# Moving the x value products behind the Wo pass, and extra parts ahead of the memory transposes and of the Wo pass, in a segmented attention kernel

## The chip, the cores and the metric

The kernel runs on one core of one Trainium2 chip. The metric is the device time of one execution in microseconds (us). "Before" is the kernel without the change, "after" the kernel with it.

## The reference, cut to what matters

```python
for s in range(64):                                 # 64 segments, one after the other
    h = concatenate([mem, x[:, 32*s:32*s+32]])      # 8 memory rows + 32 tokens, 640 features
    q, k, v = h @ Wq, h @ Wk, h @ Wv                # 32 heads of 128
    p = softmax(mask(q @ k.T * scale))
    o = (p @ v) @ Wo
    mem = o[:, :8]                                  # the next segment needs this
    outs.append(o[:, 8:])
# around it: layer norm of x, h = x + attention, then layer norm and a gated FFN with a residual
```

The 64 segments form a chain through `mem`: eight rows of scores, value products and the Wo pass have to be ready before the next projections can start. Everything else of a segment can be put into gaps of that chain.

## The kernel before

Each segment is issued in this order for TensorE (PE). The names are those of the code; the line numbers are those that the profile prints.

```python
project(a, ks, 1, (0, 1), (P2, P3), spare=20)          # K, lines 401/384; evicted to tok[0], tok[1]
dma_t(KS..., tokp[0][:, :], [("tok", 0), ("tok", 1)], [("KS",)])   # transpose of K by DMA
pv_x(s - 1, BQ[0])                                     # line 643: x value products of the LAST segment
if fin: fin()                                          # transposes of the extras' queries
norm_x(BQ[0]); trans_ox(); kx_x(q)                     # VectorE; DMA transpose ox -> oT; keys into KX
...
project(a, ks, 0, (0, 1), (P0, P1), spare=20)          # Q, evicted to tok[2], tok[3]
project(a, ks, 2, (0, 1), (P2, P3), (0, 1), spare=8)   # V, first chunks
trans8(tok[2], ..., tok[3], ..., T0)                   # line 421: token transposes of Q
kx_mem(KS[:, :, 0:M], ("KS",))                         # VectorE: memory keys into KX, needs KS
project(a, ks, 2, (0, 1), (P2, P3), (2, 3, 4), spare=12)
...
scores(s)                                              # line 540, needs KX
filler(0); filler(1)                                   # "extras": pieces of K, Q or V of other tokens,
pv_mem(s); norm_om()                                   # or of an extra Wo pass, on banks BQ
filler(2)
trans_om()                                             # line 592: memory transposes, needs om of norm_om
mask_x()
filler(3)
wo_pass(T1, MARKS[s % 4])                              # line 604: 128 matmuls, 256 instructions
to_act(s + 1, ...)                                     # VectorE: the next memory rows into act_r
filler(4)
if evac: evac()                                        # evictions of the extras
```

An instruction list in program order is kept for every engine. `MARKS` says how many PE instructions after the begin of the Wo pass a block of 256 should end (the instruction queue of before brought 201 packets for PE's 51361 matmuls and weight loads, 256 a packet), and `align` reaches that by turning some matmuls that reuse loaded weights into matmuls with a load of their own (`spare`):

```python
PE_FIRST, PE_LINE = 64, 256
MARKS = (104, 64, 92, 92)
...
if op.mark is not None:
    p = (-(at + op.mark)) % line      # instructions to add so that the mark is met
```

In this text s%4 is the class of a segment: classes 0, 1 and 2 have different extras, and the row statistics and loads of x fall into different classes too.

The softmax here doesn't subtract the row's maximum and nothing guards it: scores larger than these inputs give would overflow.

## Time and profile before

| | before |
|---|---|
| median, range of 4 runs | 1217.66 us, 1215.56 to 1220.37 |
| the profiled execution | 1211.88 us, span 1210.1, mean granted clock 0.987 |
| four segments (one of each class), segments 5 to 60 | 60.10 us |

The last row is worked out from the starts of the scores in the timeline: 841.39 us between those of segments 5 and 61, divided by 14.

The page of before: the first line gives busy time and share of every engine, the next two the busy tenths of PE and its granted clock in 40 slices, then the instruction queue (packets, MB, share), and the engines' shares of the chain of work that ended last.

```profile
PE 1110.7 (92%) x27964; PEld 529.5 (44%) x23397; DVE 641.9 (53%) x1648; ACT 328.1 (27%) x684; POOL 285.4 (24%) x567
...
PE   5589999999999999999999999999999987999998
...
PEclk9889999999999999999999999999999999999999
...
q8 instruction: 201, 3.29, 1.1%
...
PE 64%; DMA 11%; DVE 9%; POOL 7%; issue 4%; SPq 3%; ACT 2%; DVEq 0%; POOLq 0%
```

PE is busy nine tenths or more in nearly all slices, and the granted clock was 1.00 from 125 to 965 us (windows view of before). But only 64% of the last-ending chain is PE; DMA, VectorE and GpSimd hold the rest. So PE stands and waits for others, for short times and often. The waits view says for whom (line of the wait, what ended it: us in total, times, longest):

```profile
PE ps L592 <- DVE om L586: 21.1, 63, 1.1
PE ps L421 <- DVE tok L430: 19.3, 26, 1.6
PE ps L401 <- DVE act_r L518: 17.2, 63, 0.7
```

Two of these come 63 times, once at every hand-over from one segment to the next. The timeline of one segment shows their places (start, duration, engine, line, operation, tiles; in brackets the idle time and what ended it):

```profile
823.83 0.62 PE L421 MATMUL ps<-ident,tok 128*128 128x128 bf16 x8 [0.82 <-DVE tok L430]
...
825.78 0.69 PE L540 MATMUL ps<-Qr,KX 128*64 128x40 bf16 x32
...
828.45 0.28 PE L592 MATMUL ps<-ident,om 128*128 128x128 bf16 x2 [0.30 <-DVE om L586]
...
829.12 2.40 PE L604 MATMUL ps<-Wo,oT 128*32 128x160 bf16 x128
831.35 0.39 PE L401 MATMUL ps<-W,act_e 128*32 128x512 bf16 x4
831.56 0.39 PE L384 MATMUL ps<-W,act_e 128*32 128x512 bf16 x4
832.19 0.40 PE L401 MATMUL ps<-W,act_r 128*32 128x512 bf16 x4 [0.24 <-DVE act_r L518]
```

The memory transposes (line 592) stand still 0.30 us for om. Then come two extra groups, the Wo pass at 829.12, two extra groups, and the K projection of the next segment stands still 0.24 us for act_r. At 823.83 the token transposes have waited 0.82 us for tok; in this segment the Kr transpose of the extras' keys held it (VectorE stood 1.31 us for that transfer before it wrote tok at 823.08). The transposes by DMA (times, median us from issue to landing):

```profile
oT<-ox SPq DMA_TRANSPOSE x64, 2.8
KS<-tok SPq DMA_TRANSPOSE x63, 3.1
...
Kr<-tok SPq DMA_TRANSPOSE x15, 5.1
```

### The profile page before, as it was taken

Reading aid. Unit: us, or ns where it says so; the run is one execution under the profiler, and the core shown is the slowest. Engines: PE = TensorE matmul, PEld = TensorE weight load, DVE = VectorE, ACT = ScalarE, POOL = GpSimd, SP = SyncE. Lnnn points to the kernel's source line nnn. Section 1 sums busy time; section 2 is a strip of 40 time slices with the busy share of each in tenths; the row PEclk is TensorE's granted clock in tenths of the full one; section 3 lists DMA queues with packets and bytes.
Section 4 is the critical chain, followed back from the end, with each engine's and each line's share of the span. In section 5 each row is a group of like instructions: output and inputs, shape, how many; then the busy total and the mean of one; then the engine's idle time right before and its main releaser. Section 6 shows DMA issues by size and latency. Waiting matters only on the chain.

```text
span 1210.1 us, 55379 instructions
## 1 busy us (share of the span) xinstructions
PE 1110.7 (92%) x27964; PEld 529.5 (44%) x23397; DVE 641.9 (53%) x1648; ACT 328.1 (27%) x684; POOL 285.4 (24%) x567
## 2 busy tenths in 40 slices
PE   5589999999999999999999999999999987999998
PEld 2344444444444444444444444444444444443443
DVE  3245656565655565566666665565656552543522
ACT  2123232323232323232323232322232321211210
POOL 1013233323233232233232323232323220000000
PEclk9889999999999999999999999999999999999999
DMA  9933333334333434353534343434332359131200
GB/s 357 359 51 68 61 68 61 71 58 73 56 75 54 75 54 75 54 102 56 101 56 101 58 99 56 74 56 73 58 69 58 63 139 252 26 82 44 50 22 22
DMA packets 214103, 102.45 MB, mean 85 GB/s; under 512 B 188032, under 2 KB 203456, under 8 KB 213872
## 3 DMA queue, kind: packets, MB, share of 16 engines
q1 hardware_dynamic: 196016, 82.96, 31.3%
q0 software_dynamic: 17664, 15.94, 6.9%
q8 instruction: 201, 3.29, 1.1%
q14 instruction: 30, 0.25, 0.1%
q10 hardware_dynamic: 192, 0.01, 0.0%
HBM read 36.79 MB, written 7.21 MB: 36 GB/s over the span
## 4 chain that ended last, share of the span: by engine, by line
PE 64%; DMA 11%; DVE 9%; POOL 7%; issue 4%; SPq 3%; ACT 2%; DVEq 0%; POOLq 0%
PE ps L401 16%; PE ps L384 14%; PE ps L604 10%; PE ps L953 9%; POOL Vr L352 5%; DMA Kr<-tok 4%; PE ps L421 3%; PE ps L540 3%; PE ps L986 3%; DMA attn_d<-ox 3%; DMA Wo<-in_A_Wo_dram 2%; SPq L352 2%; PE ps L643 2%; DMA oT<-ox 2%; DVE ox L655 2%
## 5 line engine op out<-in xcount | busy, mean ns | idle before, releaser
L401 PE MATMUL ps<-W,act_r 128*32 128x512 bf16 x4421 | 398.1, 386 | 23.9 <-DVE act_r L518 17.2
L384 PE MATMUL ps<-W,act_r 128*32 128x512 bf16 x3459 | 339.5, 379 | 0.0
L352 POOL DMA_DIRECT2D Vr<-Vp x376 | 188.2, 508 | 481.7 <-ACT Vp L428 284.8
L401 PEld LDWEIGHTS ps<-W,act_r 128*32 128x32 bf16 x4421 | 117.3, 97 | 283.1 <-issue 158.6
L430 DVE CAST tok<-ps 128x512 bf16<-128x512 f32 x161 | 110.8, 688 | 128.7 <-PE ps L384 92.8
L604 PE MATMUL ps<-Wo,oT 128*32 128x160 bf16 x8320 | 162.9, 238 | 12.4 <-DMA Wo<-in_A_Wo_dram 8.4
L604 PEld LDWEIGHTS ps<-Wo,oT 128*32 128x32 bf16 x8320 | 150.8, 99 | 30.6 <-DVE oT L430 17.0
L428 ACT ACTIVATE tok<-ps 128x512 bf16<-128x512 f32 x161 | 96.0, 596 | 242.2 <-PE ps L384 178.4
L428 ACT ACTIVATE Qr<-ps 128x768 bf16<-128x768 bf16 (+3 forms) x110 | 69.2, 658 | 104.2 <-DVE Qr L430 92.7
L428 ACT ACTIVATE wtok<-ps 128x160 bf16<-128x160 f32 x64 | 19.5, 305 | 272.6 <-DVE TBf L517 264.5
L655 DVE TENSOR_TENSOR ox<-ps,rx 128x512 bf16<-128x512 f32 x128 | 82.5, 686 | 17.6 <-DMA attn_d<-ox 15.9
L401 PE MATMUL ps<-W,act_e 128*32 128x512 bf16 x900 | 89.0, 383 | 0.0
L384 PE MATMUL ps<-W,act_e 128*32 128x512 bf16 x900 | 88.1, 379 | 0.0
L517 DVE STREAM_TRANSPOSE TBf<-ps 128x160 f32<-128x160 f32 x64 | 22.4, 350 | 112.2 <-PE ps L604 112.1
L352 POOL DMA_DIRECT2D attn_d<-wtok x64 | 47.6, 744 | 129.1 <-ACT wtok L428 129.1
L421 PE MATMUL ps<-ident,tok 128*128 128x128 bf16 x664 | 51.1, 220 | 19.9 <-DVE tok L430 19.3
L968 DVE TENSOR_TENSOR hT<-g,ps 128x512 bf16<-128x512 bf16 (+1 forms) x56 | 38.5, 688 | 52.6 <-PE ps L953 48.7
L421 PEld LDWEIGHTS ps<-ident,tok 128*128 128x128 bf16 x664 | 37.3, 98 | 64.6 <-DVE tok L430 62.1
L953 PE MATMUL ps<-xn2T,Wg 128*128 128x512 bf16 x260 | 64.7, 379 | 0.0
L953 PE MATMUL ps<-xn2T,Wu 128*128 128x512 bf16 x260 | 64.6, 379 | 0.0
L986 PE MATMUL ps<-Wd,hT 128*128 128x320 bf16 (+1 forms) x240 | 63.3, 300 | 0.0
L430 DVE CAST Vp<-ps 128x512 bf16<-128x512 f32 x64 | 44.3, 692 | 31.6 <-PE ps L384 28.2
(91 smaller groups left out, 1138.2 us busy)
## 6 DMA issues: line engine op xcount, KB each, us to landing
Vr<-Vp POOLq DMA_DIRECT2D x124, 48.8 KB, 1.9
W<-in_A_Wk_dram SPq DMA_DIRECT2D x2, 2560.0 KB, 13.0
W<-in_A_Wq_dram SPq DMA_DIRECT2D x2, 2560.0 KB, 25.1
W<-in_A_Wv_dram SPq DMA_DIRECT2D x2, 2560.0 KB, 26.8
Wo<-in_A_Wo_dram SPq DMA_DIRECT2D x2, 2560.0 KB, 28.6
xt<-in_A_x_dram SPq DMA_DIRECT2D x30, 160.0 KB, 2.6
Vr<-Vp POOLq DMA_DIRECT2D x128, 32.5 KB, 2.3
attn_d<-wtok POOLq DMA_DIRECT2D x64, 40.0 KB, 3.2
```

The costliest lines, as they stand in the source:

```text
L352: add(eng, lambda e: e.dma_start(dst, src), r=r, w=w, dma=True)
L384: return pe.add_instruction(mybir.InstMatmult(name=nc.get_next_instruction_name(), engine=mybir.EngineType.PE, ins=[pe.lower_ap(rhs), pe.l ...
L401: ins = pe.matmul(*a, start=(c == 0), stop=(c == DC - 1), skip_group_check=True)
L421: ins = pe.matmul(bank_bf(b)[:, k * 128:(k + 1) * 128], t[:, (k % 4) * 128:(k % 4 + 1) * 128], ident[:, :], is_transpose=True)
L428: add("act", lambda a: a.activation(dst, src, ACTF.Copy), r=r, w=w)
L430: add("dve", lambda v: v.tensor_copy(dst, src), r=r, w=w)
L540: i = pe.matmul(bank((P0, P1)[e])[64 * cg:64 * cg + 64, 40 * k:40 * k + 40], KX[:, h, :], Qr[:, h, q, :], start=True, stop=True, skip_grou ...
L604: i = pe.matmul(bank(bk)[32 * gg:32 * gg + 32, 0:160], oT[:, hb, :], w[:, gg], start=(hb == 0), stop=(hb == 31), skip_group_check=True)
L655: add("dve", lambda v, kh=kh: v.tensor_tensor(ox[:, kh, :, :], src[:, :, kh, 0:128], ap(rx, kh, [[2, 4], [0, 128]]), ALU.mult), r=[B(b0 + ...
L953: ins = pe.matmul(bank(bk), w[:, c, lo:lo + 128], xn2T[par][:, c, :], start=(c == 0), stop=(c == DC - 1))
L968: add("dve", lambda v: v.tensor_tensor(hT[par][lo:128, j, :], g1[gi][lo:128, :], bank(bu)[lo:128, :], ALU.mult), r=[B(bu), ("g1", gi)], w= ...
L986: i = pe.matmul(*a, start=(j == 0), stop=(j == FC - 1), skip_group_check=True)
```

## The change

Its intent is to put work that waits for nothing where PE waited. It computes the same.

```diff
-    MARKS = (104, 64, 92, 92)
+    MARKS = (204, 164, 192, 192)
...
-            project(a, ks, 1, (0, 1), (P2, P3), spare=20)       # K
-            to_tok(P2, 0, "act")
-            to_tok(P3, 1, "dve")
+            project(a, ks, 1, (0, 1), BQ, spare=20)
+            to_tok(BQ[0], 0, "act")
+            to_tok(BQ[1], 1, "dve")
             dma_t(KS..., tokp[0][:, :], ...)
-            pv_x(s - 1, BQ[0])
-            if fin: fin()
-            norm_x(BQ[0]); trans_ox(); kx_x(q)
-            n = ...; if n: row_scale(...); dma_t(at, xt)
+            for f in late: f()                                  # row statistics put off
             project(a, ks, 0, (0, 1), (P0, P1), spare=20)       # Q
+            n = ...; if n: row_scale(...); dma_t(at, xt)
...
         filler(2)
+        filler(3)
         trans_om()
         mask_x()
-        filler(3)
+        filler(4)
+        if evac: evac()                                         # both evictions on ScalarE now
+        if woe: ...; woe_sum(BQ[0]); woe_store(...)             # by way of `at`, no longer ox
         wo_pass(T1, MARKS[s % 4] if s > 3 else None)
         to_act(s + 1, ...)
...
-        filler(4)
-        if evac: evac()
-        if woe: ...
+        pv_x(s, P0)                                             # x value products of THIS segment
+        if nfin: nfin()
+        norm_x(P0); trans_ox(); kx_x(seg_slot(s + 1))
```

Smaller things come along: half of the score matmuls load 40 instead of 64 weight columns, the row statistics of x and a residual add go to the next segment (`late`), `ln1_back` runs later, and `align` fills its `spare` places from the last one back and leaves the first four segments without a mark. The transpose of ox into oT is now queued ahead of the K transpose (KS), on the same queue, where before it followed.

More of the change, by code (lines that the diff above doesn't have):

```diff
@@ L36, in matmul, with ldweights @@
         self.n += 2
+    def ldweights(self, w):
+        self.n += 1
 class _Graph:
@@ L145, in align @@
                     at += p
-                    for o in spare:
+                    for o in reversed(spare):
                         o.spare[0] = min(p, o.spare[1])
@@ L539, in f @@
                         h = 4 * k + 2 * cg + e
-                        i = pe.matmul(bank((P0, P1)[e])[64 * cg:64 * cg + 64, 40 * k:40 * k + 40], KX[:, h, :],
+                        n = 64 - (SEG - M) * e
+                        i = pe.matmul(bank((P0, P1)[e])[64 * cg:64 * cg + n, 40 * k:40 * k + 40], KX[:, h, 0:n],
                                       Qr[:, h, q, :], start=True, stop=True, skip_group_check=True)
@@ L709, in build_kernel, with nops @@
         dma(Wo[:, 16 * i:16 * i + 16, :], A_Wo.rearrange("h e d -> e h d")[:, 16 * i:16 * i + 16, :], w=[("Wo", i)])
+    pad = [0, PE_LINE]
+    def nops(pe):
+        for _ in range(pad[0]):
+            i = pe.ldweights(ident[:, :])
+        return i if pad[0] else None
+    add("pe", nops, r=[("ident",)]).spare = pad
     row_stats(xt, ("xt",), 64)
@@ L803, in evac @@
         def evac():
-            for i, e in enumerate(("act", "dve")):
+            for i, e in enumerate(("act", "act")):
                 if j == 2:
@@ L813, in fin @@
         def fin():
-            trans8(tok[2], ("tok", 2), tok[3], ("tok", 3), P2)
-            evac_q(P2, t0, 32, 0, "act")
+            trans8(tok[2], ("tok", 2), tok[3], ("tok", 3), T0)
+            evac_q(T0, t0, 32, 0, "act")
         return part, evac, (fin if j == 0 else None)
@@ L824, in woe_sum @@
         add("act", lambda a: a.activation(tmp, bank(bk)[64:128, 0:320], ACTF.Copy), r=[B(bk)], w=[("at",)])
-        add("dve", lambda v: v.tensor_tensor(ap(ox, 0, [[1, 320]], 0, 64), tmp, bank(bk)[0:64, 0:320], ALU.add),
-            r=[B(bk), ("at",)], w=[("ox", 0), ("ox", 1)])
+        add("dve", lambda v: v.tensor_tensor(bass.AP(at, 0, [[D, 64], [1, 320]]), tmp, bank(bk)[0:64, 0:320], ALU.add),
+            r=[B(bk), ("at",)], w=[("at",)])
     def woe_store(b):
@@ L830, in woe_store @@
             dma(bass.AP(attn_d, 128 * b * D + 320 * dg, [[SEG * D, 4], [D, M], [1, 320]]),
-                ap(ox, 0, [[1, 320]], 32 * dg, 32), r=[("ox", 0), ("ox", 1)] + [("attn", 4 * b + j) for j in range(4)],
+                bass.AP(at, 32 * dg * D, [[D, 32], [1, 320]]), r=[("at",)] + [("attn", 4 * b + j) for j in range(4)],
                 w=[("attne", b, dg)], eng="pool")
-    fin = None
+    late = []
     for s in range(NSEG):
@@ L850, in build_kernel @@
             t0, nr = rider_tokens(s)
-            project(a, ks, 1, (0, 1), (P2, P3), spare=20)
-            to_tok(P2, 0, "act")
-            to_tok(P3, 1, "dve")
+            project(a, ks, 1, (0, 1), BQ, spare=20)
+            to_tok(BQ[0], 0, "act")
+            to_tok(BQ[1], 1, "dve")
             dma_t(KS[:].rearrange("p h t -> p (h t)").rearrange("p (k r) -> p k r", r=128), tokp[0][:, :],
                   [("tok", 0), ("tok", 1)], [("KS",)])
-            pv_x(s - 1, BQ[0])
-            if fin:
-                fin()
-            norm_x(BQ[0])
-            trans_ox()
-            kx_x(q)
-            n = n_rows(nb) if s % 4 == 2 and ln else 128 if e2b is not None else 0
-            if n:
-                row_scale(xt, ("xt",), n, xt, ("xt",))
-                dma_t(chunks_of(at[:, :])[:, :, 0:n], xt[0:n, :], [("xt",)], [("at",)])
+            for f in late:
+                f()
+            late = []
             if not last:
@@ L871, in build_kernel @@
                 to_tok(P1, 3, "dve")
+            n = n_rows(nb) if s % 4 == 2 and ln else 128 if e2b is not None else 0
+            if n:
+                row_scale(xt, ("xt",), n, xt, ("xt",))
+                dma_t(chunks_of(at[:, :])[:, :, 0:n], xt[0:n, :], [("xt",)], [("at",)])
             project(a, ks, 2, (0, 1), (P2, P3), (0, 1), spare=8)
@@ L879, in build_kernel @@
                 evac_k(KS, ("KS",), t0, nr, M, "dve")
-            if s % 4 == 2 and ln:
-                ln1_back(nb, chunks_of(at[:, :]), [("at",)], "pool")
             if e2b is not None:
@@ L901, in build_kernel @@
                 v_riders(t0, nr)
-        units, evac, fin = extra_units(s)
+            if s % 4 == 2 and ln:
+                ln1_back(nb, chunks_of(at[:, :]), [("at",)], "pool")
+        units, evac, nfin = extra_units(s)
         woe = s % 4 == 1 and s >= 5
@@ L914, in build_kernel @@
         filler(2)
+        filler(3)
         trans_om()
         mask_x()
-        filler(3)
-        wo_pass(T1, MARKS[s % 4])
-        to_act(s + 1, B(T1), bank(T1)[:, 0:160])
-        if s >= 1:
-            wo_rows(T1, wtok[s % 2], ("wtok", s % 2), "act")
-            store_attn(wtok[s % 2], ("wtok", s % 2), s - 1)
         filler(4)
@@ L927, in build_kernel, with f @@
             copy_op("dve", oTe[:, :, 0:M], e0, [("at",)], [("oTe", 0)])
-        if woe:
             woe_sum(BQ[0])
             woe_store(s // 4 - 1)
+        wo_pass(T1, MARKS[s % 4] if s > 3 else None)
+        to_act(s + 1, B(T1), bank(T1)[:, 0:160])
+        if s >= 1:
+            wo_rows(T1, wtok[s % 2], ("wtok", s % 2), "act")
+            store_attn(wtok[s % 2], ("wtok", s % 2), s - 1)
+        pv_x(s, P0)
+        if nfin:
+            nfin()
+        norm_x(P0)
+        trans_ox()
+        kx_x(seg_slot(s + 1))
         if s % 4 == 1 and ln:
-            row_stats(xt, ("xt",), n_rows(nb))
+            late.append(lambda nb=nb: row_stats(xt, ("xt",), n_rows(nb)))
         if s % 4 == 3 and e2 is not None:
-            add_attn(xt[:, :], xt, at, [("xt",), ("at",)], [("xt",)])
-            dma(h_d[128 * e2:128 * e2 + 128, :], xt[:, :], r=[("xt",)], w=[("h_d", e2)])
-            row_stats(xt, ("xt",), 128)
+            def f(e2=e2):
+                add_attn(xt[:, :], xt, at, [("xt",), ("at",)], [("xt",)])
+                dma(h_d[128 * e2:128 * e2 + 128, :], xt[:, :], r=[("xt",)], w=[("h_d", e2)])
+                row_stats(xt, ("xt",), 128)
+            late.append(f)
     BG, BU, BD, BT = (0, 1), (2, 3), (4, 5), (6, 7)
```

## The prediction

> **What bounds it.** TensorE's instruction stream. The page's busy table has PE at 1110.7 of 1210.1 us (92%); the granted clock is 1.00 in the steady stretches; four segments take 60.0 us, with PE busy about 56.6 (stretches view). What remains are three recurring holes on PE. I cost each from start to start in the timeline, against the shortest gap of the same pair of operations, for the 56 segments between 127 and 970 us:
>
> 1. Memory transposes wait for VectorE's normalisation: 0.68 us instead of 0.31 in 42 segments, 0.63 instead of 0.23 in 14. About 21 us.
> 2. The next key projection waits for act_r (Wo pass, VectorE transpose, copy): 0.62 instead of 0.21 in 42, 0.57 instead of 0.13 in 14. About 23.7 us.
> 3. The token transposes wait for tok: 34.5 us, floor 56 x 0.31. About 17 us. It falls in two segments of four: where the extras' Kr transpose DMA (5.1 us) holds tok, and where the Wo-e store out of ox holds norm_x (VectorE waited 15.9 us for that store).
>
> Sum about 62 us. The waits view agrees as plain idle time: 21.1 + 17.2 + 19.3 us over the run.
>
> **What the change does.** It removes no arithmetic.
> - Two extras parts (0.24 + 0.21 us each) now precede the memory transposes. The transpose starts 0.95 us after the last memory value product today; the new path is about 1.0 us long. Hole 1 closes.
> - pv_x (0.60 us of starts, plus entry and exit) stands between Wo and the next K. K starts 0.92 us after Wo's last start today; the filling is about 0.83: hole 2 shrinks to about 0.09 us, or zero where the Q extras' transposes follow.
> - Extras' evictions go to ACT before the Wo pass, so Kr's DMA starts about 2 us earlier; norm_x and kx_x leave the K-to-Q interval; the Wo-e sum uses `at` instead of ox. Hole 3 closes.
> - pv_x no longer breaks K from Q (0.31 + 0.15 becomes 0.21, with a new entry after Wo): about 4 us more.
>
> **Given back.** (a) act_r residue: 42 x 0.09, about 4 us. (b) Instruction fetch. [...] 201 packets of 16384 B on the instruction queue. A fetch starts about 0.5 us after PE enters a block, takes 0.9 to 1.6 us, and in the two stalled cases (near 1003 and 1016 us) PE ran on 1.45 us after it landed: about 3.1 us per block. Now 384 instructions (Wo, pv_x) come in about 3 us; by the new marks the block after the boundary in Wo lasts about 2.9 us in one segment of four, 3.5 in the others. Estimate: 5 us lost, and 2 in the unaligned first segments. (c) KS lands 3.1 to 3.7 us after issue, slack before the scores now 0.3 to 1 us. Estimate: 1 us.
>
> All of this lies on PE's chain and counts in full: 62 + 4 - 4 - 7 - 1, plus about 4 at the ends = 58 us.
>
> **Predicted:** 1159 us, 1146 to 1178 eight times in ten. Faster by over 2%: 0.95; within 2%: 0.04; slower: 0.01.
>
> **What shows it.** Waits of memory transposes on om, and of token transposes on tok: near 0. K on act_r: 17 us down to about 4. Four segments in about 56 us. PE busy time unchanged within 1%, its share 95 to 96%.
>
> **What would make it wrong.** KS landing later than 3.7 us, because oT's transpose now goes just ahead of it: a new wait of the scores on KX, each segment. Fetch stalls at block boundaries in every segment. VectorE late for the K eviction behind norm_x.

## The result, and the profile after

After takes 1187.73 us (median of 4, 1186.49 to 1188.26); before beside it 1217.66. The ratio is 0.9752, with a 95% interval of 0.973 to 0.9773. A ratio here is always the mean time of one kernel's fast runs over that of the other's of the same rounds, so it is not quite the ratio of the medians. The saving is 30 us, and 24 us between the two profiled executions (1211.88 and 1187.79 us). The direction was right and the size about twice too large: 1187.73 lies outside the predicted 1146 to 1178.

The same lines of the page after:

```profile
PE 1107.4 (93%) x27964; PEld 555.2 (47%) x23604; DVE 611.2 (52%) x1603; ACT 358.0 (30%) x729; POOL 279.5 (24%) x567
...
q8 instruction: 202, 3.31, 1.2%
...
PE 84%; DMA 9%; SPq 3%; issue 2%; DVE 2%; ACT 0%; DVEq 0%
```

PE's busy time is nearly what it was, and PE now holds 84% of the chain instead of 64%. The waits:

```profile
PE ps L544 <- DVE KX L433: 16.8, 19, 4.0
PE ps L404 <- issue: 11.4, 15, 2.0
...
PE ps L608 <- issue: 4.9, 10, 1.4
...
PE ps L424 <- DVE tok L433: 2.8, 2, 1.4
...
PE ps L596 <- DVE om L590: 2.6, 3, 1.1
...
PE ps L404 <- DVE act_r L521: 1.7, 1, 1.7
```

The three holes of before are closed: om 21.1 to 2.6 us, act_r 17.2 to 1.7, VectorE's tok 19.3 to 2.8 (line numbers moved by a few: 592 is 596 now, 401 is 404, 421 is 424). What is left of these lies in the opening and at the end. But there are three lines that before did not have at this size: the scores wait for KX (line 544, 16.8 us), and K and Wo wait for "issue", which is to say for nothing that the profile knows, 11.4 and 4.9 us.

Where the 24 us come from can be read from the starts of the scores: 3.7 us up to segment 5, 19.0 us between segments 5 and 61, and 1.3 us after. Four segments take 58.74 us instead of 60.10. The prediction had 54 us for that middle part and 4 for the ends, so the ends were right and the middle was 35 us short.

The next table gives the middle part by phase: mean time from the start of one group to the start of the next, by class, and the shortest such phase (the floor) that any class shows. Its numbers are worked out from the timeline of after, 14 segments per class. A column is the stretch from the scores of a segment of that class to the next scores, so its K, Q, V and token transposes, and the loads and `late` work beside them, are those of the segment after it. The classes of phases in the rest of the text are meant in this way.

| phase, us | s%4 = 0 | 1 | 2 | 3 | floor | excess of four |
|---|---|---|---|---|---|---|
| Wo to x value products | 2.42 | 2.79 | 2.33 | 2.39 | 2.33 | 0.6 |
| K to Q | 2.17 | 2.98 | 2.19 | 2.17 | 2.17 | 0.8 |
| V to token transposes | 1.00 | 1.17 | 1.05 | 1.14 | 0.97 | 0.5 |
| token transposes to scores | 1.99 | 1.95 | 2.69 | 2.22 | 1.95 | 1.1 |
| scores to memory transposes | 2.78 | 2.92 | 2.69 | 2.81 | 2.68 | 0.5 |

The sum is 3.5 us per four segments, or 49 us over the 56 segments. At the floors, four segments would take about 55.2 us; the prediction said about 56.

The first two rows are put down mostly to instruction fetch (e1 and e2 below test that): 22 stops for "issue", 12.3 us together, lie in Wo and K of these segments; for the other 8 us of the two rows the waits view books nothing. PE stops in the middle of a run of equal matmuls, and the profile shows nothing that it waited for (timeline of after, a segment of class 1):

```profile
839.86 1.56 PE L608 MATMUL ps<-Wo,oT 128*32 128x160 bf16 x78
841.86 1.07 PE L608 MATMUL ps<-Wo,oT 128*32 128x160 bf16 x50 [0.44 <-issue]
842.87 0.33 PE L647 MATMUL ps<-Vr,Px 64*32 64x129 bf16 x16
...
844.49 0.38 PE L404 MATMUL ps<-W,act_r 128*32 128x512 bf16 x2
845.61 0.39 PE L404 MATMUL ps<-W,act_r 128*32 128x512 bf16 x2 [0.74 <-issue]
```

Wo stops 0.44 us after 78 of its 128 matmuls. K starts at 844.49 and most of it comes only from 845.61. From the one stop to the other the trace has 256 instructions of PE: 99 of Wo, 128 of the value products, 29 of K. In all, 8 pairs of stops of over 0.2 us lie exactly 256 instructions apart in after. The packets of the instruction queue lie beside them. The 16 KiB packet that belongs to the second stop started at 843.01, which is 1.15 us after PE had entered its block at 841.86, took 1.31 us, and PE ran on 1.29 us after it had landed: 3.75 us for a block. The shortest block of after that lies between two such stops took 3.47 us. The whole trace agrees with a packet for every 256 instructions: 202 packets of 16384 bytes (3.31 MB) for PE's 27964 matmuls and 23604 weight loads, which is 255 a packet; in before it is 201 packets, and 256 a packet.

The fourth row is KX. Of the 16.8 us of waits, 4.0 are one wait in the last segment and 12.8 lie in the middle part. The queue of transposes, the VectorE copy that follows, and the scores, in one segment of class 2:

```profile
800.94 1.24 SPq L358 DMA_TRANSPOSE oT<-ox  x1
802.48 2.68 SPq L358 DMA_TRANSPOSE KS<-tok  x1
```

```profile
807.02 0.23 DVE L433 COPY KX<-KS 128x256 bf16<-128x256 bf16 x1 [1.39 <-DMA KS<-tok]
```

```profile
804.68 0.62 PE L424 MATMUL ps<-ident,tok 128*128 128x128 bf16 x8
...
807.30 0.63 PE L544 MATMUL ps<-Qr,KX 128*64 128x40 bf16 x32 [0.59 <-DVE KX L433]
```

The oT transpose is issued at 800.94. KS follows at 802.48, its issue alone takes 2.68 us where it took 1.23 to 1.28 on average in the classes of before, and the copy into KX stands still for it until 807.02. The scores wait 0.59 us for that copy. The transposes over the whole run:

```profile
oT<-ox SPq DMA_TRANSPOSE x64, 4.5
KS<-tok SPq DMA_TRANSPOSE x63, 3.5
...
Kr<-tok SPq DMA_TRANSPOSE x15, 4.6
```

oT took 2.8 us and takes 4.5; KS took 3.1 and takes 3.5. In before KS was issued on average 9.5 to 9.9 us after the scores, with no oT just ahead of it and the load of x, where there is one, long issued; in after it is issued at 9.8, 11.2, 10.3 and 10.7 us in the four classes. So KS is late for two reasons: it is issued 0.2 to 1.4 us later, and its own transfer is up to 0.5 us longer. In class 2, which waits most, the two are about equal (0.6 and 0.5). Four segments stand out there (31, 35, 39 and 43): a load of x and one of attention rows are issued between oT and KS (503.14 to 505.82 in the first of them), and these four hold 6.8 of the 12.8 us.

### The profile page after: what moved, and what is told of

Its sections match the earlier page's. It is cut to its first block, busy times and chain, and to the rows that moved or that the text cites. A ratio compares the mean times of both kernels' runs of the same rounds, so it can differ in the third digit from the quotient of the medians.

```text
span 1186.1 us, 55535 instructions
## 1 busy us (share of the span) xinstructions
PE 1107.4 (93%) x27964; PEld 555.2 (47%) x23604; DVE 611.2 (52%) x1603; ACT 358.0 (30%) x729; POOL 279.5 (24%) x567
## 3 DMA queue, kind: packets, MB, share of 16 engines
q8 instruction: 202, 3.31, 1.2%
## 4 chain that ended last, share of the span: by engine, by line
PE 84%; DMA 9%; SPq 3%; issue 2%; DVE 2%; ACT 0%; DVEq 0%
PE ps L404 22%; PE ps L387 19%; PE ps L608 13%; PE ps L968 10%; DMA KS<-tok 6%; PE ps L647 4%; PE ps L622 3%; PE ps L544 3%; PE ps L1001 3%; PE ps L424 3%; SPq L355 3%; DMA Wo<-in_A_Wo_dram 2%; PE ps L582 2%; PE ps L596 1%; DVE KX L433 0%
## 5 line engine op out<-in xcount | busy, mean ns | idle before, releaser
L404 PE MATMUL ps<-W,act_r 128*32 128x512 bf16 x4628 | 418.0, 383 | 20.2 <-issue 11.4
L387 PE MATMUL ps<-W,act_r 128*32 128x512 bf16 x3252 | 333.0, 379 | 0.8 <-issue 0.8
L404 PEld LDWEIGHTS ps<-W,act_r 128*32 128x32 bf16 x4628 | 142.3, 97 | 268.6 <-issue 163.8
L431 ACT ACTIVATE tok<-ps 128x512 bf16<-128x512 f32 x191 | 110.5, 595 | 290.3 <-PE ps L387 269.9
L608 PE MATMUL ps<-Wo,oT 128*32 128x160 bf16 x8320 | 167.4, 238 | 15.8 <-DMA Wo<-in_A_Wo_dram 9.1
L433 DVE CAST tok<-ps 128x512 bf16<-128x512 f32 x131 | 90.5, 691 | 139.0 <-PE ps L387 114.6
L981 ACT ACTIVATE g<-ps 128x512 bf16<-128x512 f32 (+1 forms) x56 | 32.4, 593 | 94.0 <-PE ps L968 94.0
L544 PEld LDWEIGHTS ps<-Qr,KX 128*64 128x64 bf16 (+1 forms) x2048 | 34.0, 104 | 54.9 <-DVE KX L433 46.3
L387 PE MATMUL ps<-Wd,hT 128*128 128x320 bf16 x208 | 56.9, 299 | 0.0
```

The source lines that it names most:

```text
L387: return pe.add_instruction(mybir.InstMatmult(name=nc.get_next_instruction_name(), engine=mybir.EngineType.PE, ins=[pe.lower_ap(rhs), pe.l ...
L404: ins = pe.matmul(*a, start=(c == 0), stop=(c == DC - 1), skip_group_check=True)
L431: add("act", lambda a: a.activation(dst, src, ACTF.Copy), r=r, w=w)
L433: add("dve", lambda v: v.tensor_copy(dst, src), r=r, w=w)
L544: i = pe.matmul(bank((P0, P1)[e])[64 * cg:64 * cg + n, 40 * k:40 * k + 40], KX[:, h, 0:n], Qr[:, h, q, :], start=True, stop=True, skip_gro ...
L608: i = pe.matmul(bank(bk)[32 * gg:32 * gg + 32, 0:160], oT[:, hb, :], w[:, gg], start=(hb == 0), stop=(hb == 31), skip_group_check=True)
```

## The experiments

15 kernels were run in four batches. Each batch ran on one chip and had its own runs of before, so that medians of different batches are compared by their ratios. All results are correct against the reference. Each diff is against after unless it says otherwise.

| run | median us | ratio to before [95%] | four segments us |
|---|---|---|---|
| after | 1187.73 | 0.9752 [0.973, 0.9773] | 58.74 |
| e1_marks_up | 1166.61 | 0.9597 [0.9574, 0.962] | 57.22 |
| e2_oldmarks | 1211.41 | 0.9968 [0.994, 0.9995] | 60.20 |
| e3_ks_first | 1207.08 | 0.9936 [0.9902, 0.9971] | 59.69 |
| e4_late | 1201.14 | 0.9884 [0.986, 0.9909] | 59.66 |
| e5_ks_first_ote | 1175.07 | 0.9685 [0.9647, 0.9723] | 57.64 |
| e6_e5_marks | 1163.81 | 0.9595 [0.9559, 0.9631] | 56.95 |
| e7_loads | 1177.93 | 0.9707 [0.9662, 0.9751] | 58.19 |
| e8_filler | 1198.13 | 0.9883 [0.9837, 0.9929] | 59.13 |
| e9_stats_wo | 1170.71 | 0.9608 [0.9588, 0.9628] | 57.39 |
| e10_marks_m8 | 1181.40 | 0.9692 [0.9675, 0.9708] | 58.08 |
| e11_marks_m16 | 1178.84 | 0.9674 [0.9653, 0.9694] | 58.17 |
| e12_store_late | 1195.02 | 0.9815 [0.9793, 0.9836] | 59.10 |
| e13_delay_oT | 1226.27 | 1.0064 [1.0009, 1.0118] | 60.87 |
| e14_delay_after_oT | 1254.00 | 1.0277 [1.0224, 1.0331] | 62.94 |
| e15_mix | 1169.08 | 0.9569 [0.9516, 0.9623] | 57.27 |

The theory after reading the trace: the missing 35 us are instruction fetch (about 1.1 us per four segments more than predicted) and the late KS (about 1.4 more, with the value products that wait after it). The rival: most of it is the floors, that is, the new order is not worth what the idle time promised, and the two waits would be replaced by others if they were taken away.

### Fetch: e1_marks_up and e2_oldmarks

```diff
# e1_marks_up
-    MARKS = (204, 164, 192, 192)
+    MARKS = (231, 188, 214, 222)
# e2_oldmarks
-    MARKS = (204, 164, 192, 192)
+    MARKS = (104, 64, 92, 92)
```

> Only the alignment marks change: the boundary of the 256-instruction blocks inside each Wo pass lies about 20 to 30 instructions later (231, 188, 214, 222 instructions after the pass begins). Theory F (part of the missing gain is waiting for instruction blocks, about 3.5 us per block when the block before is dense): in the segments with the Wo-e products the stall in K (0.84 us or more each, 14 times) goes, a stall of about 0.4 us inside Wo stays, the other segments gain 0.1 to 0.2 us of stall: 1178 to 1185 us, from 1187.7. Rival (the gaps are waits for data, the marks do not matter): 1187 to 1188 us, gaps at the same instructions as before.

> The changed kernel with the marks of the kernel before (104, 64, 92, 92), so the second block boundary falls at the end of the x value products and start of K. Theory F: the block then holds the rest of Wo and the x value products, about 2 us of work against 3.5 us of fetch, so a stall of about 1.4 us in each of 56 segments in place of 1.5 us per four: about 60 us more, 1240 to 1255 us, slower than the kernel before the change. Rival (the marks do not matter): 1187 us.

e1 moves nothing but where the blocks of 256 instructions begin (through `align`, 23582 weight loads instead of 23604), and takes 1.6% off (1166.61 us), more than expected. Its waits:

```profile
PE ps L544 <- DVE KX L433: 11.8, 13, 4.8
...
PE ps L608 <- issue: 3.1, 7, 1.5
...
PE ps L404 <- issue: 2.5, 3, 2.0
```

The waits of K for "issue" fell from 11.4 to 2.5 us and those of Wo from 4.9 to 3.1, and the KX wait fell as well, from 16.8 to 11.8. K to Q in class 1 is 2.28 us instead of 2.98. Per four segments the two fetch phases lose 0.8 us less, and the two phases behind KX (token transposes to scores, scores to memory transposes) 0.55 us less. So fetch is a cause of lost time, and a part of the KX wait hangs on it.

e2 keeps the marks that were tuned for the order of before. Then a block ends in the value products behind Wo, in all classes:

```profile
PE ps L647 <- issue: 61.5, 61, 3.5
...
PE ps L544 <- DVE KX L433: 4.0, 5, 1.8
```

61 stops of 1 us on average (0.6 to 1.4 in the middle part) are a direct measurement of what one badly placed block costs here. Counted from the mark in Wo, the 56 blocks of the middle part that end in such a stop took 2.8 to 3.6 us, median 3.1: the fetch started 0.6 us after PE had entered the block (median), sooner than in after. Yet the kernel is only 24 us slower than after, not 52 to 67. In the middle part the new stops cost 62 us; 20 us come back because the stops in Wo and K are gone, which is only the same loss in another place, and 21 us because the KX wait, the value products and the token transposes no longer lose theirs: the KX wait falls from 16.8 to 4.0 us. That the pause gives the transposes the time that they lacked fits this. It was the first sign that the waits of this kernel hide each other.

### KX: e3_ks_first, e5_ks_first_ote, e7_loads and e4_late

```diff
# e3_ks_first: oT's transpose, and the loads of x and attention rows, are queued behind KS
-        if s % 4 == 3 and e2 is not None: dma(xt, x_ap...); load_attn(at, e2, ...)
-        if s % 4 == 0 and ln and e2b is None: ln1_load(nb, xt, ("xt",))
...
             dma_t(KS..., tokp[0][:, :], ...)
+            trans_ox()
+            if s % 4 == 3 and e2 is not None: dma(xt, x_ap...); load_attn(at, e2, ...)
+            if s % 4 == 0 and ln and e2b is None: ln1_load(nb, xt, ("xt",))
...
         norm_x(P0)
-        trans_ox()
# e7_loads: the same for the loads only; oT's transpose stays ahead of KS
# e5_ks_first_ote: e3, and VectorE's copy out of oT behind the exponentials
-            copy_oTe(s - 1)                    # (or its variant into `at`)
             to_v(P3, Vp, 1, ("Vp",), "dve")
             scores(s)
             exp_mem()
+            copy_oTe(s - 1)
# e4_late: the deferred row statistics behind Q's evictions instead of ahead of them
-            for f in late: f()
             project(a, ks, 0, (0, 1), (P0, P1), spare=20)
             to_tok(P0, 2, "act"); to_tok(P1, 3, "dve")
+            for f in late: f()
```

> The transpose DMA of oT and the loads of x rows are queued behind the key transpose DMA (KS) instead of ahead of it; nothing else moves. Theory Q (scores wait because KS stands behind them in the queue): KS issues up to 1 us sooner and lands about 3.1 us after issue, the scores' wait on KX (16.8 us in the waits) falls under 3 us, the excess of the second memory value product (about 5 us) mostly too: 1169 to 1176 us. Rival (KS is late because K itself ends late, or because the Kr transpose and the stores share the DMA engines): KX wait stays above 10 us, 1183 to 1188 us.

> The deferred row statistics and the residual add on VectorE go behind the eviction of the Q projection instead of ahead of it. Theory L (they delay that eviction and so the token transposes): the token transposes' wait on tok (4.7 us, one VectorE and one ScalarE cause) falls to about 0 to 2 us, total 1183 to 1186 us. Rival (that wait comes from something else): no change, 1187 to 1188 us.

e3 was a miss: 1207.08 us, slower than after.

```profile
PE ps L404 <- issue: 13.9, 17, 2.0
PE ps L582 <- ACT Vp L431: 10.3, 47, 0.5
PE ps L582 <- DVE Pbd L557: 10.3, 15, 1.5
...
PE ps L544 <- DVE KX L433: 8.3, 5, 4.7
```

The KX wait halved, as meant (16.8 to 8.3), but the memory value products (line 582) now wait 20.6 us for Vp and Pbd. oT lands later, and VectorE's copies out of oT, which stand just ahead of the eviction of V in its list, now wait 43.8 us for it in 60 waits. The wait was moved, not removed. e4 was a miss too: 1201.14 us, the KX wait rose to 20.0 us and K's stops for "issue" from 11.4 to 15.8. The statistics need two activations of ScalarE (a logarithm and an exponential), `row_scale` on VectorE waits for them (18.8 us in 28 waits, 8.7 in 13 in after), and the copy into KX stands behind `row_scale` in VectorE's list. Why K stops more often was not traced.

> The run with the key transpose first moved the wait: scores no longer waited, but VectorE's copy of oT into oTe (or e0) stands before the eviction of V and waited for the later oT transpose, and the memory value products waited for V. Here the key transpose and the oT transpose keep that order (key first, loads of x last) and that copy moves behind VectorE's work on the memory scores. Theory Q2 (the queue order was right, the copy's place was the new wait): scores wait on KX under 4 us, memory value products wait under 3 us in all, time 1170 to 1178 us. Rival (whatever is taken away on the queue comes back elsewhere): 1187 us or more.

> Only the loads of x rows go behind the key transpose; oT stays ahead of it. It concerns one segment in four, whose scores wait 0.26 us on average and whose key transpose issues 0.6 us later than the others. If the load in front is the cause there, that wait goes: 1182 to 1185 us. Rival (oT in front is the cause): 1187 us.

The KX line of e5, then that of e7:

```profile
PE ps L544 <- DVE KX L433: 9.1, 5, 5.2
```

```profile
PE ps L544 <- DVE KX L433: 6.3, 10, 2.5
```

e5 takes VectorE's copy out of the way as well, and 1175.07 us is where it was expected. By the ratios that is 0.7% better than after. Its KX wait is 9.1 us in 5 waits: 5.2 in the last segment, and 3.9 in the four segments where the deferred residual add stands ahead of the copy into KX on VectorE. In the other 52 segments of the middle part no KX wait is left. e7 shows that a part is had by the loads alone: 0.9707 against 0.9752, with overlapping intervals, and 1177.93 us is faster than was expected; its KX wait is 6.3 us. Both classes with a load between oT and KS gain in the phase to the scores: class 3 falls from 2.22 to 1.96 us, and class 2, with the four segments named above, from 2.69 to 2.27. So the position of KS in the queue is a cause. By the whole times it is worth less than fetch (0.7% and 1.6%); by the phases of the traces it is not: e5 takes 15 us off the two phases behind KX, e1 takes 12 us off the two fetch phases and 8 off those behind KX.

### Both together: e6_e5_marks

```diff
# e5_ks_first_ote, and
-    MARKS = (204, 164, 192, 192)
+    MARKS = (231, 188, 214, 222)
```

> Both repairs at once: the queue order with the copy behind the memory scores, and the marks 231, 188, 214, 222. If the two losses are separate (fetch about 1 us per four segments saved, KX and its followers about 1.4), the time is 1150 to 1156 us; if they feed on each other (a fetch stall hides the KX wait), about 1160.

```profile
PE ps L544 <- DVE KX L433: 8.7, 5, 3.7
...
PE ps L404 <- issue: 2.8, 3, 2.0
...
PE ps L608 <- issue: 2.1, 5, 0.5
```

e6 takes 1163.81 us, ratio 0.9595, near the 1160 of the case that the two feed on each other. If the two causes were separate, the gains would add: 1.6% and 0.7%, so about 0.953. They do not add; e6 is as fast as e1 alone within the intervals (in the traces its middle part is 3.9 us shorter). This fits an order of the queue that matters only as long as fetch stops leave KS late; no run separates it further. Both versions beat both kernels of the change.

### What the pause was worth: e8_filler

```diff
         filler(2)
-        filler(3)
         trans_om()
         mask_x()
+        filler(3)
         filler(4)
```

> One part of the change undone: the second of the two extras parts goes back behind the memory transposes, all else as changed. The prediction costed the wait before the transposes at 0.37 us in 42 segments and 0.4 in 14, 21 us. If it counts in full: 1206 to 1210 us. If the pause also gives the instruction fetch time, so that stalls inside Wo go (about 8 us): 1198 to 1203 us.

```profile
PE ps L596 <- DVE om L590: 21.1, 63, 1.1
```

Undoing this part of the change brings hole 1 back exactly: 21.1 us in 63 waits, the line of before. The kernel takes 1198.13 us, the lower edge of what was expected if the pause also gives fetch its time. The ratio rises by 1.3% (0.9752 to 0.9883), which is 16 us of before, and the medians of the two batches differ by 10.4; four segments are 0.39 us longer, which over 14 is 5.5 us in the middle part. Each of these is less than the 21 us that had been booked for this hole, though the ratios with their intervals leave room for about 10 to 22. The trace of the middle part says where the rest goes: with the pause back, Wo to the value products takes 2.32 us instead of 2.42 and 2.39 in classes 0 and 3 and 2.41 instead of 2.79 in class 1 (8 us in all), and the phase to the scores in class 2 falls from 2.69 to 2.45 (4 us over all classes).

### The rest of the best version: e9_stats_wo, e10_marks_m8, e11_marks_m16 and e15_mix

```diff
# e9_stats_wo: e6, `late` removed; row statistics and residual add on VectorE in Wo's window
         mask_x()
+        if s % 4 == 1 and ln: row_stats(xt, ("xt",), n_rows(nb))
+        if s % 4 == 3 and e2 is not None: add_attn(...); dma(h_d..., xt...); row_stats(xt, ("xt",), 128)
# e10_marks_m8:  e9 with MARKS = (223, 180, 206, 214)
# e11_marks_m16: e9 with MARKS = (215, 172, 198, 206)
# e15_mix: e6, only the s % 4 == 3 line moved to Wo's window
```

> Both repairs (queue order with the copy moved, marks 231, 188, 214, 222) and the row statistics and the residual add put on VectorE behind the masks, where it waits about 1.6 us for the Wo pass. The trace of both repairs shows four segments that lose about 2 us each because the deferred residual add and statistics stand ahead of the Q eviction and of the KX copy. Theory L2 (the place, not the work, costs): those four lose nothing, and the token transposes' 0.1 us in one segment of four goes: 1152 to 1156 us against 1163.8. Rival (as in the earlier failed move of the statistics, it costs elsewhere): 1163 us or more.

> The same with the marks 8 instructions lower (223, 180, 206, 214): less stall inside Wo, more in K of the Wo-e segments. If the optimum is flat, within 3 us of its sibling.

> The same with the marks 16 lower (215, 172, 198, 206): each 8 instructions of K are 0.29 us, so the Wo-e segments' stall in K grows to about 0.6 us while Wo's falls by about 0.1: 2 to 6 us slower than the best sibling.

> The best version so far (key transpose first, oTe copy later, marks up; 1163.8 us, ratio 0.9595), with the deferred residual add of four segments moved from the K projection to the window of the Wo pass, and the row statistics of the other segments left where they are (moving both was slower in one class: K waited for act_r in 13 segments, 6.3 us). The four segments that lose about 2 us each should lose about 0.5: 6 us less, ratio 0.954 to 0.957. If the add delays act_r instead, ratio 0.958 to 0.961.

e9 did what it was to do in class 3 (token transposes to scores 2.33 to 1.96 us) and gave it back in class 1, where K waits for act_r again, because the statistics stand ahead of the copy into act_r on VectorE:

```profile
PE ps L404 <- DVE act_r L521: 6.3, 13, 1.7
PE ps L544 <- DVE KX L433: 5.7, 2, 5.2
```

In sum it is not to be told from e6 (0.9608 and 0.9595), although the phase from V to the token transposes lies at its floor in all classes but one (1.00 there). e15 moves only the four segments with the residual add: 0.9569, in the expected range, but its interval covers that of e6, so no gain is shown. e10 and e11, with marks 8 and 16 instructions lower, are 0.9% and 0.7% slower than e9, more than was expected of either; in e11 a projection stops for "issue" 14 times on line 387, for 10.2 us. A few instructions of shift are worth 8 to 11 us. No rule for the best mark came out of these runs.

### Why oT takes 4.5 us: e12_store_late, e13_delay_oT and e14_delay_after_oT

```diff
# e12_store_late: the store of the attention rows (GpSimd queue) behind the next value riders
-            store_attn(wtok[s % 2], ("wtok", s % 2), s - 1)
+            held.append((wtok[s % 2], ("wtok", s % 2), s - 1))   # issued behind v_riders
# e13_delay_oT: three transfers of 128 bytes ahead of oT's transpose
         norm_x(P0)
+        for i in range(3): dma(spare_d[i:i + 1, :], ox[0:1, 0, 0, 0:64], ...)
         trans_ox()
# e14_delay_after_oT: the same three behind it
```

> The changed kernel with one move: the store of attention rows is issued after the V riders of the next segment instead of right after the Wo pass. Theory D (oT's transpose lands 4.1 to 4.6 us after issue instead of 2.8, and so delays KS behind it, because that store shares the DMA engines with it at that moment): oT lands in about 3 us, KS issue is not blocked, KX wait falls under 8 us, 1175 to 1182 us. Rival (oT is slow for another reason): oT stays above 4 us, 1186 to 1189 us.

What the trace of after shows of theory D: the store was issued 1.31 us (median) ahead of oT's transpose, and packets of its queue (q0) ran during the transpose in all 55 segments from 5 to 59. The page books the packets of every queue as a share of the same 16 DMA engines (q1 36.0%, q0 6.8%, q8 1.2%), and names no packet's engine. e12 was a miss for both theories: 1195.02 us, and oT's transpose still took 4.3 to 4.6 us on average in classes 1 to 3. The store is not what slows it.

What goes with it was found by laying the packets of the instruction queue beside the transposes. The next table counts oT transposes of segments 5 to 59. The time is from the issue to the last of the transpose's 4-byte completion packets; that is about 0.5 us less than the landing the profile gives, and can be had for every run. "Hit" means that an instruction packet began 0.5 to 2.0 us after the issue; "free" that one began between 1 us before and 0.5 us after it, or none did between 1 us before and 3 us after.

| run | hit: number, median us | under 2.75 us | free: number, median us |
|---|---|---|---|
| before | 0 | | 32, 2.31 |
| after | 41, 3.89 | 0 | 3, 2.27 |
| e1_marks_up | 12, 3.69 | 0 | 14, 2.47 to 2.51 |
| e2_oldmarks | 0 | | 55, 2.28 to 2.32 |
| e5_ks_first_ote | 0 | | 53, 2.44 |
| e7_loads | 36, 3.55 | 0 | 4, 2.29 |
| e8_filler | 48, 3.58 | 0 | 0 |
| e12_store_late | 28, 3.91 | 0 | 5, 2.30 |
| e13_delay_oT | 27, 3.46 | 0 | 28, 2.29 to 2.73 |
| e14_delay_after_oT | 27, 3.78 | 7 | 6, 2.27 |

(Where two groups of free transposes are put together, both medians are given. The rest of each 55 had a packet that began later than 2.0 us; they were short in before and mostly in e14, and long in after, e7 and e8 and mostly in e1 and e12. So the bounds of "hit" are not where the effect ends.)

A transpose that is hit takes 0.7 to 1.6 us more than a free one of the same run, in the six kernels that have both. Of the runs not in the table, e11 does not fit the split: 8 of its transposes, of those whose landing the trace gives, had a packet between 0.5 us before and 0.2 us after the issue and would count as free, but they landed after 3.7 to 4.5 us, where those without a packet near them took 2.8 to 3.0. e2 moved the blocks and kept the queue's order, e5 kept the marks and moved oT: both took oT out of the hits, and both made it short. It fits the lower KX wait of e1 too: in class 2, 10 of the 11 oT transposes whose landing the trace gives took 2.9 to 3.3 us instead of 4.1 to 5.1, and the phase from the token transposes to the scores fell from 2.69 to 2.30 us. Then two kernels were made to test it.

> After, with three tiny transfers (128 bytes out of ox) queued just ahead of oT's transpose, so that the transpose is issued some 1.2 to 1.8 us later; the instruction stream of TensorE is untouched, so its fetches stay where they are. Collision theory: oT's transpose takes 4.5 us in after because an instruction fetch begins 0.5 to 2.2 us after its issue in 54 of 59 segments. Delayed, the fetch lies before or right at the issue: oT lands 2.8 to 3.1 us after its issue in at least 40 of 63 segments, and the key transpose behind it 3.0 to 3.3 us after its own in most. Rival (oT is slow whenever it goes first, fetch or no fetch): 4.3 to 4.6 us as before. Time: the delay pushes the key transpose back by about as much as it saves, so 1184 to 1197 us under the collision theory, over 1197 under the rival.

(Counted again in the trace of after, a packet began 0.5 to 2.2 us after the issue in 47 of the 59 segments from 1 to 59, not in 54; 55 of them have one 0.6 to 2.6 us after it.)

> Control for the run before: the same three tiny transfers, queued just behind oT's transpose instead of ahead of it. oT is issued where after issues it, so the fetch still falls into it. Both theories: oT still lands about 4.5 us after its issue. If the tiny transfers themselves sped oT up, it would land in 2.8 here too. The key transpose is issued up to 1 us later than in after: 1190 to 1205 us.

```profile
PE ps L545 <- DVE KX L434: 35.1, 39, 2.5
```

```profile
PE ps L545 <- DVE KX L434: 53.2, 40, 4.8
```

The three transfers delayed oT by only 0.9 to 1.1 us, not 1.2 to 1.8. 18 of 55 transposes were under 2.75 us where after has 3, not the 40 expected; all of the 27 that were still hit were long. The control did not hold still either: its slower segments moved oT against the blocks, 31 of 55 were short, and 7 of them although hit. So the split by hit or free is strong in every run of the table but graded at its edges (in e13 the 21 with a packet just at the issue took 2.73 us, the 7 with none 2.29), the pair made for it is not a clean proof, and how a fetch delays a transpose was not shown. The packets show which part came late: oT's transpose ends with 32 completion packets, and in the 11 of after whose fetch began 2.0 to 3.0 us after the issue, 30 of them were there at 2.28 us (median), as in a free one, and only the last two came 0.9 to 1.4 us later. So 2 of the 32 were late there, not all of them.

The pair showed something else more sharply. KS was issued 0.7 to 1.1 us later than in after in e13, and 0.8 to 1.8 us later in e14, and they are 3.2% and 5.4% slower than after (by ratios), with 35.1 and 53.2 us of KX waits. The segment has no slack left for KS. That is probably also why neither fell into its expected range.

## Why the prediction was right or wrong, point by point

- **"Hole 1 closes", "hole 2 shrinks", "hole 3 closes": right.** The three lines of the waits view went from 21.1, 17.2 and 19.3 us to 2.6, 1.7 and 2.8. The act_r residue that the prediction kept (about 4 us) is zero in the steady part.
- **"PE busy time unchanged within 1%": right** (1110.7 and 1107.4). Its share was to be 95 to 96% and is 93%, as the span is longer than predicted.
- **"About 4 at the ends": near** (5.0; with the 2 us of (b) in the first segments taken off, 2 were to be expected).
- **"(b) Instruction fetch. Estimate: 5 us lost, and 2 in the unaligned first segments": one of the two steps that failed, in its size.** In the 56 steady segments the two phases that fetch stretches are 1.5 us per four above their floors, so 20 us. The block that lasts "about 2.9 us in one segment of four" was foreseen: it runs from the boundary in Wo to the one in K of class 1, and without its stop it does take 2.9 to 3.0 us. Its need was taken as 3.1 us from two stalled cases, in which the fetch starts about 0.5 us after PE enters the block. In after the fetch starts 1.04 us after (median over all blocks; in before it was 0.26), and stalled blocks took from 3.47 us up, mostly 3.5 to 3.8. So K of class 1 lost 0.8 us per four instead of 0.2. The losses inside Wo (0.6 us per four) stand in no term of their own there. The 3.1 us are not wrong everywhere: they are the median of e2's stalled blocks, where the fetch starts at 0.6 us. Why it starts later in after stays open.
- **"(c) KS ... Estimate: 1 us": the other mis-sized term, and as large.** The phase to the scores lost 1.1 us per four, and the value products after it 0.5, so about 21 us. The prediction named it under "what would make it wrong", with the right cause (oT's transpose goes ahead). What it lacked: oT's own time does not stay at 2.8 us (4.5 in after, where a fetch falls into 41 of 55 of its transposes), and loads stand between oT and KS: one in class 3, two in four segments of class 2.
- **"All of this lies on PE's chain and counts in full": wrong as a rule.** e8 put back a hole of 21.1 us and lost 10 to 16. e2 put 62 us of stops into the middle part in place of 20 us of other fetch losses, and that part grew by 20 us and not by 42. A pause of PE is not only lost time here: with e8's pause back the phases of Wo lost 8 us less, and with e2's stops the KX wait was 4.0 us instead of 16.8. When the pauses were taken out, these were paid for elsewhere.
- The 0.5 us per four between V and the token transposes were in no term of the prediction. No wait of after accounts for all of it, but the runs do: the new marks alone leave 0.3 (e1), and with the deferred residual add, or that and the row statistics, out of the way as well 0.1 and 0.0 are left (e15, e9). So it came from fetch and from `late`.

The account: 54 us were predicted for the middle part and 19 measured. Against the prediction, fetch took 15 us more (20 for 5), KX and what follows 20 more, and the token transposes 7; the act_r residue gave 4 back. That is 38, for 35 missing, or 37 if the 2 us of the first segments are counted outside the middle part, where they lie; the rest is within the rounding of floors and estimates.

## What to carry to other kernels

The idle time had paid for two things, and where idle time is removed from an instruction stream like this one they are worth a recount: the time that every block of instructions has until the next has to be there (20 us were lost in the two phases of fetch, where 5 were estimated), and the slack of every transfer whose queue order changes (21 us, where 1 was estimated). Idle times of one engine did not add up to a saving here: 62 us of holes were costed, and 24 us came between the two profiled executions. Take out one and look at which of the others grows. The placement of block boundaries, by hand in this kernel, had to be tuned again with the change of order: it was worth as much (1.6%) as two thirds of the change itself.
